# Pooled softmax in three exponentials, a normalisation in four pieces that sorts the heads, and a newly written order

## The chip, the cores and the metric

One Trainium2 chip, one core of it. The metric is the device time of one execution in microseconds (us), the median of several runs. Engines are named as the profile names them: PE is TensorE (matmuls), PEld its weight loads, DVE is VectorE, ACT is ScalarE, POOL is GpSimd, SP is SyncE, which here only issues DMAs.

## The reference

Eight heads of attention over 576 positions, for 8 batches, in two branches that are added; the sum goes through a gated feed-forward layer.

```python
# attention, head_dim 64, factor 4
q_d = q.reshape(B, H, Sd, 4, D).mean(axis=3)      # k_d, v_d likewise: 144 pooled rows
out_d = softmax(q_d @ k_d.T / 8) @ v_d            # pooled branch
out_up = np.repeat(out_d, 4, axis=2)
mask = np.abs(pos[:, None] - pos[None, :]) < 4    # local branch: a band of 7
out_local = softmax(where(mask, q @ k.T / 8, -1e9)) @ v
x = (out_up + out_local)                          # 8 x 576 x 512
# feed-forward with token shift
x_prev = shift of x by one position
xk = mu_k * x + (1 - mu_k) * x_prev;  xr = mu_r * x + (1 - mu_r) * x_prev
v = np.maximum(xk @ w_k, 0) ** 2 @ w_v            # w_k 512 x 1024, w_v 1024 x 512
out = sigmoid(xr @ w_r) * v                       # w_r 512 x 512
```

The weights and mu come as 64-bit floats and are turned into 32-bit floats on the chip, each as a high part and a low part (`weight_scale`, `weight_shift`, `weight_tail`, `weight_sign`, `weight_high`, then `weight_diff` and `weight_left`, or `weight_low` on GpSimd).

## The kernel before

Attention goes by **tiles**: tile n is a pair of heads of one batch, 32 tiles in all, four to a batch. A tile's q and k are loaded (`load_raw`), brought into the layout with head_dim on the partitions (tiles 0 to 4 by `flip` on PE, with copies out by `turn_part` on ACT and DVE; later ones by DVE), pooled on GpSimd (`pool_q`, `pool_k`) and multiplied: `score_both` for tiles 0 to 4, `run_pe` from tile 5 on, which also does the value products of the tile before. The pooled scores and the local scores of a tile share one PSUM tile of two banks, the board `ps_a`, of which there is one: the next tile's scores can start only when all readers of the last one are through (`score_top`, `down_top` on DVE, `down_exp` on ACT).

The **pooled probabilities** of a tile are 2 heads x 144 queries x 144 keys. Queries 0 to 127 of the two heads and the last 16 of each are spread over three column blocks of the board; the two halves of its first and third block belong to different heads. `down_exp` (line 744) takes five exponentials, four over 64 partitions, so that in `ad` each block of columns holds one head; each also sums its rows. `down_sum` forms reciprocals on DVE, `down_norm` (line 755) multiplies on GpSimd in place. Then `ad` is transposed into `adT`: for tiles 0 to 7 by PE (`down_turn`, lines 763 to 767, one PSUM bank) with one copy out on ACT (`down_copy`, line 792); from tile 8 on by DVE in 32 x 32 blocks (`down_blocks`, line 773) and by DMA through DRAM (`down_out`, `down_in`). `av_pe` (or `run_pe`) multiplies `adT` with the pooled v.

The **feed-forward layer** goes by 18 chunks of 256 rows: `k_pe` (x w_k), `r_pe` (x w_r) and `v_pe` (the squares x w_v) are the large matmuls on PE; between `k_pe` and `v_pe` stand `k_part`, `k_sum`, `k_relu`, `k_high`, `k_low` on ACT, DVE and GpSimd. Chunk 0 needs all four tiles of batch 0, whose mix with the row before is done by `mix_pe`, `mix_split`, `mix_rest`. So the program has a **first stretch**, up to the first `k_pe` (line 974), in which tiles 0 to 3 and the weights are prepared, and a long rest in which chunks and tiles are woven together.

The **order** of all 2,417 steps is written out in a string, `ORDER`: each engine gets its steps in just that order, SP's DMA issues among them. `Plan.arrange` reads the string, and with durations given in the `add(...)` calls works out which PSUM bank each step uses, where matmuls without use (`keep_warm`, line 483) are put into PE's gaps, and for which earlier transfer an early DMA issue has to wait (`landed_before`, with `QUEUE`). These durations set no time on the chip, but by way of banks, filling and waits they shape the program.

Of the kernel before, what the change touches and what calls it, by code (L numbers as in the profile page):

```python
# [52 lines left out]
494A1k3c1s3d1$0$3=3e3s1l1t3f1%1&3u3>404B4C1a413#4D1(1b3v1c4s4E4t4F4u1)1m1*3$1,1v4G4I4M4Q4J3%3w4K4H1-1w1x1y5l4N
1d5n4L3t3x1.1/3y5i5,3j5k5-5.3&5m4O4P4R4S3(4T1e4v5o5p3)4w5u4x4Y4g4U4V4k4c4W1z1!4X4l3z4m4Z3*3!1:1;4y4d4z6I5j6J5r
5$5w5s4a5%4b4e4f4n4*5t5v5:6M5<4!4#5x4h4+4$5y5;5z5q4%5&5(5)4o554p5!565*5>1f5=4i4j4,5#5+61574&4-6B6j4q4.4r4<6O6C
6N656D4(6E4)4/62666P4:51585T6359676m6k606Q68694=4>6A6K6#6n6l6F6G6H6$5/5A644;52505S5U536o6q6p6S6y6L6z956c6W6&54
6R6d6!5C5D5G5K5V6X6(6Y6Z6e6r5H5E6T6a5W6f6s6g6*6%6h6)6U6V5F6t6b6i6u6v5X5I5L5M6w5J5N6+6,6-6.785Y5Z5O969293949X9V
9Y6x6/7198797A7B7C7D5P7G5Q7E5R977F725a5b5c7H7I737J6:746;7K6<7N7T7O7U7V7P5d7x7Z7l7L5B9y9U5e5g9v99759E9A767Q7R7S
7M6=777W7a867X9B7b7c879H7Y6>7f7d9C9D7g9F7h9N7e7-9W9z5f709G9Z88898A7i7j7m7n8D9I9O7k7o9P9Q7/7p7q9J8E7,7.9a9b7:9R
9S9K9c7r7;7%7s8B9T8F7t7y7u7<9d7z8C7v7w8G9L7&7!7(9o7)7#7*8H9!7$9i8J8P7=8K9e9f8L7+9g8b7>8V80A4A7A89M9p9$9w9hCS9q  # L60
9r9s9#8Q8M9j9k9t9%8N8R8O9u9&8I9l9x8S8T8W8U9m8X9<8c9(8Y8Z818d839=9)8a8h8e8f8i8j8+8k8lAA8n9,828gA6A59n9+AC8o9>8p
A08mA9A19-9.A2AB8,8z8-8t9*A39/AD9:AOAP8u8q8rAEAF8v8wAG8sAV8xAWAQ8!AXAYAZAdCU8#Ae8$Af8yARAaAIAb8.8/8)8:8(8;Ag8%
# [1349 lines left out]
```

## Time and profile before

| | us |
|---|---|
| median of 3 runs (681.16 to 681.96) | 681.39 |
| the profiled execution | 680.52 |
| its span, first to last instruction | 678.7 |
| PE busy in the span | 648.4 |
| first `k_pe` starts at | 81.52 |

The span lacks 1.82 us of the profiled execution's time, which lie around it; the median is 0.87 us above that execution. A PE record of this kernel is one pass of a matmul: a 32-bit product shows as two records (x2 in the count), a product of rounded operands (fp32r) as one. [...]

### The profile page before, as it was taken

The numbers are of one execution on the slowest core, as the hardware profiler recorded it, in microseconds if no ns is written. First come the engines' busy times: TensorE is split into PE (matmuls) and PEld (weight loads), VectorE is DVE, ScalarE is ACT, GpSimd is POOL, SyncE is SP. The second block draws the span as 40 slices with busy tenths as digits, with TensorE's granted clock in tenths as the row PEclk, the third lists the DMA queues.
The fourth block names the chain that finished last, engine by engine and source line by source line (L and its number), as shares of the span: only waits on it lengthen the run. The fifth ranks groups of instructions, "written<-read, shape, count | busy, mean of one in ns | idle before, by whom it ended". The sixth has DMA issues, their size and how long they took to land.

```text
span 678.7 us, 19065 instructions
## 1 busy us (share of the span) xinstructions
PE 648.4 (96%) x7292; PEld 539.6 (79%) x7292; DVE 514.7 (76%) x1044; ACT 488.9 (72%) x1275; POOL 284.2 (42%) x375
## 2 busy tenths in 40 slices
PE   5886999999999999989999999999998999999997
PEld 5565898987888888868788888888887888888885
DVE  3888765679997998898978878789799876664312
ACT  3887697678886887958686777688777686765543
POOL 5435587664354456452444444544445242000000
PEclk9897999999999999999999999999999999999999
DMA  8999434646554457645245444664564133000101
GB/s 290 242 297 201 79 72 72 147 91 137 105 98 82 87 138 149 145 82 125 56 95 121 96 89 100 140 132 101 108 137 96 34 88 80 1 17 1 46 1 62
DMA packets 251580, 71.97 MB, mean 106 GB/s; under 512 B 224346, under 2 KB 243170, under 8 KB 251490
## 3 DMA queue, kind: packets, MB, share of 16 engines
q1 hardware_dynamic: 251490, 70.76, 46.3%
q8 instruction: 57, 0.93, 0.6%
q14 instruction: 33, 0.27, 0.2%
HBM read 56.85 MB, written 13.86 MB: 104 GB/s over the span
## 4 chain that ended last, share of the span: by engine, by line
PE 72%; DVE 12%; ACT 7%; SPq 2%; issue 2%; DMA 2%; POOL 1%; DVEq 0%; POOLq 0%; ACTq 0%
PE acc L1040 23%; PE ps_g L978 14%; PE ps_r L1024 13%; PE ps_g L980 7%; PE ps_v L802 5%; PE ps_a L654 2%; ACT ad L744 2%; PE ps_g L974 2%; PE ps_a L723 1%; DVE kk L991 1%; PE ps_a L659 1%; DVE kl L1013 1%; DVE xk L957 1%; DVE dx L957 1%; PE ps_w L476 1%
## 5 line engine op out<-in xcount | busy, mean ns | idle before, releaser
L1040 PE MATMUL acc<-wv,kh 128*128 128x512 f32 x578 | 182.8, 397 | 0.4 <-DVE sig L1050 0.2
L978 PE MATMUL ps_g<-xk,wk 128*128 128x512 f32 x512 | 140.7, 396 | 3.8 <-DVE xk L966 3.2
L1040 PEld LDWEIGHTS acc<-wv,kh 128*128 128x128 f32 x578 | 101.0, 189 | 17.9 <-DVE sig L1050 0.7
L978 PEld LDWEIGHTS ps_g<-xk,wk 128*128 128x128 f32 x512 | 92.8, 188 | 26.4 <-issue 4.5
L1040 PE MATMUL acc<-wv,kl 128*128 128x512 f32 x289 | 113.3, 392 | 0.0
L1024 PE MATMUL ps_r<-wr,xr 128*128 128x512 f32 x432 | 105.8, 394 | 2.9 <-DVE kk L991 2.9
L1024 PEld LDWEIGHTS ps_r<-wr,xr 128*128 128x128 f32 x432 | 79.9, 188 | 21.2 <-DVE kk L991 1.9
L1013 DVE TENSOR_TENSOR kl<-kk,kh 128x256 fp32r<-128x256 f32 x119 | 61.7, 521 | 33.6 <-ACT kh L1006 33.5
L980 PEld LDWEIGHTS ps_g<-xk,wk 128*128 128x128 f32 x512 | 78.1, 188 | 11.0
L991 DVE TENSOR_TENSOR kk<-ps_g,kk 128x256 f32<-128x256 f32 x128 | 52.5, 413 | 44.0 <-ACT kk L986 43.7
L986 ACT ACTIVATE kk<-ps_g 128x256 f32<-128x256 f32 x128 | 47.6, 377 | 51.5 <-PE ps_g L980 30.3
L980 PE MATMUL ps_g<-xk,wk 128*128 128x256 f32 x512 | 81.1, 281 | 0.0
L1000 ACT ACTIVATE kk<-kk 128x256 f32<-128x256 f32 x128 | 52.3, 412 | 37.7 <-DVE kk L991 37.1
L744 ACT ACTIVATE ad<-ps_a,mxd 64x144 f32<-64x144 f32 (+1 forms) x160 | 60.2, 376 | 11.1 <-DVE mxd L736 6.5
L682 POOL TENSOR_TENSOR sm<-sm,mx 128x384 f32<-128x384 f32 x28 | 25.7, 917 | 99.4 <-DVE mx L677 91.0
L1006 ACT ACTIVATE kh<-kk 128x256 fp32r<-128x256 f32 x144 | 60.2, 418 | 7.2 <-PE acc L1040 2.7
L1040 PEld LDWEIGHTS acc<-wv,kl 128*128 128x128 f32 x289 | 54.2, 188 | 13.1 <-DVE kl L1013 0.5
L1013 POOL TENSOR_TENSOR kl<-kk,kh 128x256 fp32r<-128x256 f32 x25 | 18.8, 754 | 108.1 <-ACT kh L1006 107.9
L1005 ACT ACTIVATE kk<-kk 128x256 f32<-128x256 f32 x144 | 59.3, 412 | 2.1
L618 POOL TENSOR_TENSOR tk<-kz 64x288 f32<-64x288 f32 (+1 forms) x56 | 43.3, 773 | 28.8 <-DVE kz L562 9.3
L697 POOL TENSOR_TENSOR sm<-sm,ssum 128x384 f32<-128x384 f32 x32 | 29.2, 911 | 54.5 <-DVE ssum L693 50.3
L802 PE MATMUL ps_v<-bd,vw 64*64 64x48 f32 x1536 | 51.7, 219 | 0.0
(134 smaller groups left out, 1273.7 us busy)
## 6 DMA issues: line engine op xcount, KB each, us to landing
vw<-in_v_dram SPq DMA_DIRECT2D x126, 96.0 KB, 2.7
out_dram<-sig SPq DMA_DIRECT2D x35, 256.0 KB, 2.2
v<-in_v_dram SPq DMA_DIRECT2D x32, 256.0 KB, 3.0
qraw<-in_q_dram SPq DMA_DIRECT2D x108, 72.0 KB, 2.5
kraw<-in_k_dram SPq DMA_DIRECT2D x108, 72.0 KB, 2.4
wk<-in_moe_w_k_dram SPq DMA_DIRECT2D x8, 512.0 KB, 4.8
wv<-in_moe_w_v_dram SPq DMA_DIRECT2D x8, 512.0 KB, 5.3
keys<-blocks SPq DMA_DIRECT2D x96, 40.0 KB, 1.9
```

The source lines that it names most:

```text
L744: nc.scalar.activation(ad[h, x, 0:144], ps[h, t, :], AF.Exp, scale=1.0 / 128, bias=mx[h, t:t + 1], accum_out=sd[h, x:x + 1])
L802: nc.tensor.matmul(pv[r][64 * e:64 * e + 64, cols], lhs, rhs, start=(i == 1), stop=(i == NG + 1 + (r != e)))
L978: nc.tensor.matmul(ps, w_k_part(p, f, 0), x[:, :, p, :], start=(p == 0), stop=False)
L980: nc.tensor.matmul(ps[:, 0], w_k_part(p, f, 1), x[:, 0, p, :], start=False, stop=(p == NP - 1))
L986: nc.scalar.activation(kk, ps[:, 1], AF.Copy)
L991: nc.vector.tensor_tensor(out=kk, in0=ps[:, 0], in1=kk, op=ALU.add)
L1000: nc.scalar.activation(kq[c, f], kq[c, f], AF.Relu)
L1005: nc.scalar.activation(kk, kk, AF.Square)
L1006: nc.scalar.activation(kh, kk, AF.Copy)
L1013: eng.tensor_tensor(out=kl, in0=kk, in1=kh.bitcast(F32), op=ALU.subtract)
L1024: nc.tensor.matmul(ps, x[:, y, p, P * t:P * t + P], ws[f"r{p}"][:, w, :], start=(m == 0), stop=(m == len(mm) - 1))
L1040: nc.tensor.matmul(accs[c][t][:, h], x[:, P * t:P * t + P], ws[f"v{f}"][:, w, h], start=(f == 0 and m == 0), stop=(f == NF - 1 and m == 2) ...
```

## The change

1. `down_exp` takes three exponentials, each over all 128 partitions, with the heads left as they stand in the board.
2. `down_norm` takes four multiplications on GpSimd in place of one, and writes to another tile, `an`, where they put the heads in order (64 partitions x 2 x 144, twice 64 x 144, 128 x 144). `clear` zeroes `an` in place of `ad`.
3. `down_turn` (tiles 0 to 7) uses full 128-column turns and two PSUM banks: 4 transposes of 128 x 128 and 3 small matmuls, where 8 matmuls were, 4 of them on 64 columns. `down_copy` takes three activations in place of one.
4. Durations of the plan are changed, and `ORDER` is another.
5. A wait of `store_mul` on the gate is spelled out for the last chunk's halves.

```diff
-        for t, x, h in ((0, 0, slice(0, 64)), (0, 1, slice(64, P)), (2, 1, slice(0, 64)), (2, 0, slice(64, P)), (1, 2, slice(0, P))):
-            nc.scalar.activation(ad[h, x, 0:144], ps[h, t, :], AF.Exp, scale=1.0 / 128,
-                                 bias=mx[h, t:t + 1], accum_out=sd[h, x:x + 1])
+        for t, x in enumerate((0, 2, 1)):
+            nc.scalar.activation(ad[:, x, :], ps[:, t, :], AF.Exp, scale=1.0 / 128,
+                                 bias=mx[:, t:t + 1], accum_out=sd[:, x:x + 1])
...
-        sd, x = st[n]["sd"], ad[:, :, 0:144]
-        nc.gpsimd.tensor_tensor(out=x, in0=x, in1=sd[:, :, None].broadcast_to([P, 3, 144]), op=ALU.mult)
+        sd = st[n]["sd"]
+        lo, hi = slice(0, 64), slice(64, P)
+        for h, to, of in ((lo, slice(0, 2), slice(0, 2)), (hi, 0, 1), (hi, 1, 0), (slice(0, P), 2, 2)):
+            x, y, z = an[h, to, 0:144], ad[h, of, :], sd[h, of] if of != 2 and h is lo else sd[h, of:of + 1]
+            z = z[:, :, None].broadcast_to([64, 2, 144]) if h is lo else z.broadcast_to([x.shape[0], 144])
+            nc.gpsimd.tensor_tensor(out=x, in0=y, in1=z, op=ALU.mult)
...
-        for e in range(2):
-            nc.tensor.matmul(ps[:, e, 0:128], ad[:, e, 0:128], idn, start=True, stop=True)
-            nc.tensor.matmul(ps[:, e, 128:144], ad[:, 2, 0:128], lasts[e], start=True, stop=True)
-        for e in range(2):
-            nc.tensor.matmul(ps[64 - 64 * e:128 - 64 * e, 2, 0:128], ad[:, e, 80:144], idn, start=True, stop=True)
-            nc.tensor.matmul(ps[64 - 64 * e:128 - 64 * e, 2, 128:144], ad[:, 2, 80:144], lasts[e], start=True, stop=True)
+        for x, ps in enumerate(d["ps_t"]):
+            o = [(16, 80), (0, 0)][x == 0]
+            for e in range(2):
+                nc.tensor.transpose(ps[:, e, 0:128], flat[:, DP * e + o[e]:DP * e + o[e] + 128], idn)
+            if x == 0:
+                nc.tensor.matmul(ps[:, :, 128:144], flat[:, 2 * DP:2 * DP + 128], lasts, start=True, stop=True)
+            else:
+                for e in range(2):
+                    nc.tensor.matmul(ps[:, e, 128:144], flat[:, 2 * DP + o[e]:2 * DP + o[e] + 128], lasts[:, e], start=True, stop=True)
...
-        nc.scalar.activation(adT, st[n]["ps_t"], AF.Copy)
+        for x, ps in enumerate(st[n]["ps_t"]):
+            for e in range(x + 1):
+                h = slice(0, P) if x == 0 else slice(64 - 64 * e, P - 64 * e)
+                nc.scalar.activation(adT[h, 0:2] if x == 0 else adT[h, 2], ps[h] if x == 0 else ps[h, e], AF.Copy)
...
-011<0X001=242625290f2T2U212X02092y0H2V1S0P0.1>201L2W2z1E173B0Y0Z2207230g0h272R2Z282a0i0a0j0b2Y2d082b0A2B2I2c2C
+001<2101221=0X2T2U0f0224092X2y2z0H1>1L0.1E0P202V3B230Y250827282a2Z0g260Z0a2Y0b030h2c0i0j292B2$2d2R070c2b2f040A
```

Where the new order moves things, by the built programs:

PE up to and at tile 2's scores. `kraw` and `qraw` with `ps_f` are the flips of k and q; `ps_a<-kd,qd_71` opens the scores of an even tile, `qd_72` of an odd one; `ps_w` are weights. Before, at tile 2 (the row ahead is the end of tile 1's value products):

```order
L802 MATMUL ps_v<-bd,vw 64x48 x9
L553 MATMUL ps_f<-idn,kraw 64x64 x18
L935 MATMUL ps_m<-xt,diag 128x256 x4
L553 MATMUL ps_f<-idn,qraw 64x64 x18
L717 MATMUL ps_a<-kd,qd_71 128x144
L649 MATMUL ps_a<-mask_77,idn 128x192 x2
```

Now, from the end of tile 0's scores to the opening of tile 1's:

```order
L724 MATMUL ps_a<-kd,qd_71 64x144 x4
L554 MATMUL ps_f<-idn,qraw 64x64 x18
L554 MATMUL ps_f<-idn,kraw 64x64 x18
L477 MATMUL ps_w<-w_244,idn 128x512
L478 MATMUL ps_w<-wk_339,nidn 128x512
L477 MATMUL ps_w<-w_251,idn 128x512
L478 MATMUL ps_w<-wv_365,nidn 128x512
L718 MATMUL ps_a<-kd,qd_72 128x144
```

Tile 2's k was flipped behind the value products of tile 1; now it is flipped ahead of the scores of tile 1, and tile 2's scores stand directly behind the value products of tile 0. All of PE's steps ahead of the first `k_pe` are the same ones as before, without the 9 filling matmuls, which the new program doesn't have.

SP at the program's start. `wk` and `wv` are weights of 512 KB, `qraw` and `kraw` 288 KB each (tiles 0, 1, 2 in turn), `idn` and `mask_77` constants of 64 and 96 KB. Before:

```order
L502 DMA qraw<-in_q_dram 128x576
L447 DMA wk_100<-in_moe_w_k_dram 128x1024
L390 DMA mask_77<-in_band_dram 128x6x32
L391 DMA idn<-in_ident_dram 128x128
L502 DMA kraw<-in_k_dram 128x576
L447 DMA wv_132<-in_moe_w_v_dram 128x1024
L502 DMA qraw<-in_q_dram 128x576
L502 DMA kraw<-in_k_dram 128x576
L395 DMA bd<-in_moe_mu_k_dram 4x128
L396 DMA bd<-in_moe_mu_r_dram 4x128
L447 DMA wk_180<-in_moe_w_k_dram 128x1024
L502 DMA qraw<-in_q_dram 128x576
```

Now:

```order
L392 DMA idn<-in_ident_dram 128x128
L503 DMA qraw<-in_q_dram 128x576
L503 DMA kraw<-in_k_dram 128x576
L448 DMA wk_126<-in_moe_w_k_dram 128x1024
L503 DMA qraw<-in_q_dram 128x576
L503 DMA kraw<-in_k_dram 128x576
L448 DMA wv_132<-in_moe_w_v_dram 128x1024
L396 DMA bd<-in_moe_mu_k_dram 4x128
L397 DMA bd<-in_moe_mu_r_dram 4x128
L448 DMA wk_156<-in_moe_w_k_dram 128x1024
L503 DMA qraw<-in_q_dram 128x576
L503 DMA kraw<-in_k_dram 128x576
```

The constants (the mask is one row above) go first, no weight stands ahead of tile 0's q and k, and tile 2's k follows its q at once; before it came 14 rows later.

GpSimd at tile 0's normalisation; `sm` is the local branch, `tk`, `kd` the pooling of k, `v` and `vd` that of v. Before:

```order
L697 TENSOR_TENSOR sm<-sm,ssum 128x384
L618 TENSOR_TENSOR tk<-kz_76 128x288
L619 TENSOR_TENSOR kd<-tk 128x144
L755 TENSOR_TENSOR ad<-ad,sd 128x3x144
L627 TENSOR_TENSOR v_82<-v_82 128x3x128
```

Now:

```order
L698 TENSOR_TENSOR sm<-sm,ssum 128x384
L761 TENSOR_TENSOR an<-ad,sd 64x2x144
L761 TENSOR_TENSOR an<-ad,sd 64x144 x2
L761 TENSOR_TENSOR an<-ad,sd 128x144
L619 TENSOR_TENSOR tk<-kz_75 128x288
```

One multiplication became four, and tile 2's pooling of k (`kz_75`) stands right behind them.

## Rows read from the trace of the kernel before

**Rows 1.** The page: span, PE's busy time, DMA throughput in 40 slices of 17 us.

```profile
span 678.7 us, 19065 instructions
...
PE 648.4 (96%) x7292; PEld 539.6 (79%) x7292; DVE 514.7 (76%) x1044; ACT 488.9 (72%) x1275; POOL 284.2 (42%) x375
...
GB/s 290 242 297 201 79 72 72 147 91 137 105 98 82 87 138 149 145 82 125 56 95 121 96 89 100 140 132 101 108 137 96 34 88 80 1 17 1 46 1 62
```

**Rows 2.** Waits of PE: line, what it waited for, us, times, longest.

```profile
PE ps_f L553 <- DMA kraw<-in_k_dram: 7.3, 1, 7.3
PE ps_a L717 <- POOL kd L619: 3.6, 1, 3.6
PE ps_g L978 <- DVE xk L966: 3.2, 4, 1.4
...
PE ps_r L1024 <- DVE kk L991: 2.9, 2, 1.5
```

**Rows 3.** Busy time by stretch: length, engines, granted clock, DMA share, GB/s; sum to 82.

```profile
54.00:58.00 4.00, 2.08 (x10) 1.64 (x10) 3.90 (x11) 3.92 (x13) 1.93 (x3) 0.50 0.96 296
...
sum 82.00, PE 63.84 PEld 49.66 DVE 59.04 ACT 56.90 POOL 40.45; mean PE 2.78 PEld 2.16 DVE 2.57 ACT 2.47 POOL 1.76
```

**Rows 4.** The same view, one stretch in the long rest.

```profile
280.00:320.00 40.00, 37.58 (x310) 30.73 (x303) 37.25 (x66) 29.87 (x73) 14.29 (x17) 1.00 0.55 112
```

**Rows 5.** Timeline of PE: start, us, line, operation, records, idle before in brackets.

```profile
14.61 0.48 PE L717 MATMUL ps_a<-kd,qd 128*128 128x144 f32 x2 [0.33 <-ACT qd L610]
...
24.98 0.68 PE L717 MATMUL ps_a<-kd,qd 128*128 128x144 f32 x2
...
28.14 0.49 PE L763 MATMUL ps_t<-idn,ad 128*128 128x128 f32 x2
...
29.59 1.20 PE L483 MATMUL ps_x<-nidn 128*128 128x512 f32 x4
...
42.05 1.11 PE L553 MATMUL ps_f<-idn,kraw 64*64 64x64 f32 x32
...
46.51 0.51 PE L717 MATMUL ps_a<-kd,qd 128*128 128x144 f32 x2
...
55.92 0.84 PE L717 MATMUL ps_a<-kd,qd 128*128 128x144 f32 x2 [3.57 <-POOL kd L619]
...
81.52 10.28 PE L974 MATMUL ps_g<-xk,wk 128*128 128x256 f32 x84
```

**Rows 6.** Timeline of ACT: two exponentials of tile 0 and its one copy out.

```profile
19.65 0.38 ACT L744 ACTIVATE ad<-ps_a,mxd 64x144 f32<-64x144 f32 x1 [0.48 <-DVE mxd L736]
...
20.13 0.38 ACT L744 ACTIVATE ad<-ps_a,mxd 64x144 f32<-64x144 f32 x1
...
29.71 0.53 ACT L792 ACTIVATE adT<-ps_t 128x432 f32<-128x432 f32 x1 [2.00 <-PE ps_t L767]
```

**Rows 7.** Timeline of GpSimd: tile 1's pooled k, tile 0's normalisation.

```profile
22.16 0.43 POOL L619 TENSOR_TENSOR kd<-tk 128x144 f32<-128x144 f32 x1
22.59 0.91 POOL L755 TENSOR_TENSOR ad<-ad,sd 128x432 f32<-128x432 f32 x1
```

**Rows 8.** Groups by form: line, engine, shapes, count, busy us, mean ns, idle before.

```profile
L1013 DVE TENSOR_TENSOR kl<-kk,kh 128x256 fp32r<-128x256 f32 x119 | 61.7, 521 | 33.6 <-ACT kh L1006 33.5
...
L618 POOL TENSOR_TENSOR tk<-kz 64x288 f32<-64x288 f32 x48 | 36.0, 750 | 14.2 <-DVE kz L591 6.3 <-DMA keys<-blocks 4.0 <-DVE mxd L736 1.7
```

**Rows 9.** Line 1013 alone: duration min/median/max in ns, first and last start.

```profile
L1013 DVE TENSOR_TENSOR kl<-kk,kh x119: 361/426/1123, 112.1 to 670.9; 128x256 fp32r<-128x256 f32 x119
```

**Rows 10.** SP's issues: start, us; k of tiles 2 and 3.

```profile
25.00 0.40 SPq L502 DMA_DIRECT2D kraw<-in_k_dram  x1
...
33.72 0.33 SPq L502 DMA_DIRECT2D kraw<-in_k_dram  x1
```

**Rows 11.** Tile ad between 388 and 425 us: normalisations, and the transposes that read them.

```profile
L755 POOL TENSOR_TENSOR ad<-ad,sd x2: 910/952/995, 394.2 to 413.6; 128x432 f32<-128x432 f32 x2
L773 DVE STREAM_TRANSPOSE blocks<-ad x2: 662/670/678, 403.3 to 422.3; 128x480 f32<-128x480 f32 x2
```

More of the change, by code (lines that the diff above doesn't have):

```diff
@@ L53 @@
[L53 to L62, printed above, removed]
@@ L114 @@
     TAIL = dict(PE=0.16, DVE=0.08, ACT=0.095, POOL=0.04, SP=0.0)
-    WAIT = dict(PE=0.055, DVE=0.035, ACT=0.035, POOL=0.1, SP=0.1)
+    WAIT = dict(PE=0.16, DVE=0.035, ACT=0.035, POOL=0.1, SP=0.1)
     SAME = 0.033
@@ L118 @@
     TABLES = dict(down_exp=1, score_exp=1, gate=2)
-    ISSUE, LAND = 0.6, 1.1
-    GROW = dict(DVE=1.03, ACT=1.02, POOL=1.06, SP=1.1)
-    QUEUE = 6.0
+    ISSUE, LAND = 0.6, 2.2
+    GROW = dict(DVE=1.02, ACT=1.02, POOL=1.04, SP=1.08)
+    QUEUE = 4.5
     SLACK = 1.0
@@ L421, in clear @@
     def clear():
-        for x in (*kzs, *qTs, *qds, *v4s, side, ad):
+        for x in (*kzs, *qTs, *qds, *v4s, side, an):
             nc.gpsimd.memset(x, 0.0)
@@ L1094, in prepare @@
             for nm in "qk":
-                add("PE", 1.1, R - 9.5, flip, n, nm, r=[f"{nm}raw{n}", "idn"], new=[(f"{nm}flip{n}{x}", "bank") for x in range(2)])
+                add("PE", 1.35, R - 9.5, flip, n, nm, r=[f"{nm}raw{n}", "idn"], new=[(f"{nm}flip{n}{x}", "bank") for x in range(2)])
                 for x in range(2):
-                    add(*(("ACT", 0.45) if (nm, x) in FLIPACT else ("DVE", 0.45)), R - 9, turn_part, n, nm, x,
+                    add(*(("ACT", 0.68) if (nm, x) in FLIPACT else ("DVE", 0.68)), R - 9, turn_part, n, nm, x,
                         r=[f"{nm}flip{n}{x}"], w=[(f"{nm}T{i}", x)])
@@ L1115, in down_steps @@
         add("DVE", 0.8, R1 - 14, down_top, n, r=[ps], w=[f"mxd{n}"], lock=ps)
-        add("ACT", 2.0, R1 - 13, down_exp, n, r=[ps, f"mxd{n}"], w=["ad"], lock=ps)
+        add("ACT", 1.2, R1 - 13, down_exp, n, r=[ps, f"mxd{n}"], w=["ad"], lock=ps)
         add("DVE", 0.36, R1 - 10, down_sum, n, r=["ad"], w=[f"sd{n}"])
-        add("POOL", 0.91, R1 - 9, down_norm, n, r=[f"sd{n}"], w=["ad"])
+        add("POOL", 1.75, R1 - 9, down_norm, n, r=[f"sd{n}", "ad"], w=["an"])
         if n < EARLY:
-            add("PE", 1.0, R1 - 7, down_turn, n, r=["ad"], new=[(f"pst{n}", "bank")])
-            add("ACT", 0.5, R1 - 6, down_copy, n, r=[f"pst{n}"], w=["adT"])
-        else:
-            add("DVE", 0.62, R1 - 7, down_blocks, n, r=["ad"], new=[(f"blk{n}", "dtmp")])
-            add("SP", 3.0, R1 - 6.5, down_out, n, r=[f"blk{n}"], w=[f"keys{n % 2}"], dma=1.9)
+            add("PE", 0.95, R1 - 7, down_turn, n, r=["an"], new=[(f"pst{n}{x}", "bank") for x in range(2)])
+            add("ACT", 0.9, R1 - 6, down_copy, n, r=[f"pst{n}0", f"pst{n}1"], w=["adT"])
+        else:
+            add("DVE", 0.67, R1 - 7, down_blocks, n, r=["an"], new=[(f"blk{n}", "dtmp")])
+            add("SP", 3.0, R1 - 6.5, down_out, n, r=[f"blk{n}"], w=[f"keys{n % 2}"], dma=1.5)
     def score_steps(n):
@@ L1253, in s_part @@
                 for i in range(n):
-                    add("DVE", 0.67 / n, where["v7"] - 6, store_mul, c, t, i, r=[f"acc{c}.{t}"],
+                    add("DVE", 0.67 / n, where["v7"] - 6, store_mul, c, t, i, r=[f"acc{c}.{t}"] + ([f"sig{c}.{t}"] if n > 1 else []),
                         w=[f"sig{c}.{t}"] if n == 1 else [(f"sig{c}.{t}", i)])
@@ L1293, in attention_moe @@
         score_steps(n)
-        add("PE", 1.35, after(n), av_pe, n, **av_of(n))
+        add("PE", 1.5, after(n), av_pe, n, **av_of(n))
         value_steps(n)
@@ L1326, in attention_moe @@
                     prepare(EARLY)
-                    add("PE", 0.9, at_run[n] + 1, down_alone, EARLY, **join(down_of(EARLY), dict(new=[("psx", "att")])))
+                    add("PE", 1.4, at_run[n] + 1, down_alone, EARLY, **join(down_of(EARLY), dict(new=[("psx", "att")])))
                     down_steps(EARLY, "psx")
```

106 lines of the change are left out of this document (59 added, 47 removed).

## The prediction

> **What bounds the kernel now.** First the page: PE is busy 648.4 of 678.7 us [rows 1]. A quicker ACT or a slower GpSimd counts only where PE waits, and all waits together are 30 us. So the next view is PE's list of waits [rows 2], and then PE's timeline, to see where they lie [rows 5]. There are three places. (a) The start: 7.3 us until the first q and k have landed. (b) The first stretch, up to the first `k_pe` at 81.52. By the sum of its stretches PE is busy 63.84 us of the first 82 [rows 3], so some 18 us are idle, 7.3 of them the start and about 10.7 inside; the longest gap inside is 3.57 us ahead of tile 3's scores at 55.92 [rows 5], where PE waits for GpSimd's pooled k. [...] (c) The rest, 81.52 to 678.7: 597.2 us with only some 7 us of waits (3.2 on `xk`, 2.9 on `kk` and smaller ones [rows 2]) and the last store's way out. The rest is bound by PE's work, which the change leaves nearly as it is. The first stretch is a chain of dependent steps, and it is there that an order can gain much.
>
> In PE's timeline the scores of tiles 0 to 3 open at 14.61, 24.98, 46.51 and 55.92, and the first `k_pe` stands at 81.52 [rows 5]: spacings of 10.4, 21.5, 9.4 and 25.6 us. The odd one is the second. Tile 2's k was issued at 25.00 [rows 10] and flipped at 42.05 [rows 5], behind the value products of tile 1, because SP's and PE's rows stand so.
>
> **Part 1, the new order, first stretch.** I follow the five pieces of that sum through the new queues with durations of this trace.
>
> - *Start.* Ahead of tile 0's k there were 1,248 KB (q, a weight, two constants, k), now 736. At 290 GB/s in the first slice [rows 1] the 512 KB less are 1.8 us, so PE starts at about 5.5 in place of 7.3. Score 0 opens as much earlier, and by another 1.5 us at most, since `turn_sign` and a weight have moved behind tile 0 on ACT: 11.3 (bounds 10.8 and 13).
> - *Score 0 to 1.* Tile 1 waits for the board, and its last reader is `down_exp`, 0.48 us from one exponential to the next [rows 6]. Two fewer save 0.96 us. The weight steps around it are much the same: 10.4 becomes 9.4. Opens at 20.7.
> - *Score 1 to 2.* Tile 2's q and k are flipped before score 1 now, so only the board holds score 2 back, as it did score 1: about 9.4 us for 21.5. Opens at 30. Its loads come in time: up to tile 2's k 3.4 MB are asked for, and the first slice alone moves 290 GB/s x 17 us = 4.9 MB [rows 1].
> - *Score 2 to 3.* Here part of that comes back. ACT and DVE must still do the weights and diagonals that filled the gap. On ACT, 19 steps stand between tile 1's and tile 2's exponentials, which I put at 13 us, and tile 3's q is copied out behind them and pooled (0.67 + 0.43 us) after that: about 17 us, against 9.4. Opens at 47. Tile 3's k (issued at 33.72 before [rows 10]) has 8.0 MB up to it now; two slices move 290 and 242 GB/s [rows 1], so 8.0 MB are there by about 30.
> - *Score 3 to the first `k_pe`.* Readers of the board on DVE, exponentials, reciprocals, four multiplications, turn, copies, value products, scores of tile 4, the last mix: the steps are those of before, with 0.96 us less on ACT, 1.1 more on GpSimd (part 2) and two more small copies. Before, PE held tile 3's turn back behind value products and a weight that came late; these stand clear now. I take 20.5 us for 25.6.
>
> Sum: 11.3 + 9.4 + 9.4 + 17 + 20.5 = 67.6. [...] A walk like this leaves out small waits, so I add 2.5 and take **70.0** (bounds 65 and 80) for 81.52: **-11.5 us**.
>
> **Part 2, the pieces.** ACT: two exponentials fewer, 0.48 us each [rows 6], in 32 tiles: 31 us of its 489 [rows 1]; worth nothing by itself where PE doesn't wait. GpSimd: one multiplication of 0.91 us [rows 7] becomes one like the 64 x 288 of line 618, 0.75 [rows 8], and three like the pooled k's last step, 0.43 [rows 7]: 2.04 us, so +1.1 us in each tile, 36 us in all. Bounds: +0.9 if neighbours overlap, +1.5 if they are slowed. In the first stretch this cancels ACT's gain; later it is hidden by slack. In the late trace the normalisation starts at 394.2 and its reader, the transpose, at 403.3 [rows 11]: 8.1 us between end and use; the next pair is alike (413.6, 422.3). Copies out of early turns: one of 0.53 [rows 6] becomes three; about +0.6 in 8 tiles, in ACT's time freed. The turn on PE took 29.59 - 28.14 = 1.45 us [rows 5]; the new one has 4 transposes, which no row shows, and 3 small products: between 1.0 and 1.9, and I take no change. Banks: a turn asks for two of six, for 2 to 3 us, at nothing.
>
> GpSimd's added time has one more way to cost. Line 1013's subtraction on DVE takes 426 ns in the median, 521 in the mean and up to 1,123 [rows 8, 9], and GpSimd works beside it: 0.095 x 119 = 11 us lost there. If twice that is lost over all such lines with 284 us of GpSimd [rows 1], 36 us more cost some 3 us of DVE, and PE sees a part. [...]
>
> **Part 3, the rest.** PE's work after the first `k_pe` is the same, and so is the tail. Of the 7 us of waits there I expect new ones in place of old: DVE is at 37.25 of 40 us in 280 to 320, where PE loses 2.4 [rows 4]. The new order asks for `r_pe` of chunk 0 about 4 us earlier than before while GpSimd has two weights more to do than at that point before, of 1.3 us each. I take **+1 us** (bounds -4 and +6).
>
> **Sum.** 680.52 - 11.5 + 1 = 670.0 for a profiled execution; the median before is 0.87 above it: **671.0**.
>
> **The rivals.**
> 1. *The first stretch shrinks, and half is lost again in chunks 0 and 1*, because weights and loads that the gap gave time for are late: PE then waits on GpSimd's `weight_low` or on k's low parts. For it: GpSimd gets fuller. Against: 40.45 of 82 us are its load now [rows 3]. 677, range 674 to 680.
> 2. *Nothing is gained, since loads bound the first stretch.* For it: 290, 242, 297 and 201 GB/s in the first four slices [rows 1], then 79: all of the weights come in that time, and tiles asked for earlier push weights back. Against: the bytes up to tiles 2 and 3, above. 681, same.
> 3. *Slower: the four multiplications come onto each tile's path.* If the new order puts the transpose or the turn right behind the normalisation, 1.1 us reach PE in 27 tiles (5 to 31): +30 us, or 701 with the gain of the start; it decides from where the 8.1 us of slack [rows 11] is used up, and it makes the kernel slower from 11 of these tiles on. [...]
> 4. *Better:* the first `k_pe` stands near 65, with PE at its full clock throughout: 665.
>
> **How the numbers follow.** Forecast (666 to 675) 0.60; rival 1 0.17; rival 2 0.07; rival 3 0.10; rival 4 0.06. The range 664 to 680 holds the forecast and rivals 1 and 4. Within 0.2% (680.0 to 682.8) is about what a measurement can't tell from no change. Faster: 0.60 + 0.06 + 0.16 = 0.82; same: 0.07 + 0.01 = 0.08; slower 0.10.
>
> **What would show it.** Right: the first `k_pe` (now line 987) at 66 to 74; scores of tiles 2 and 3 near 30 and 47; three exponentials of 0.48 us spacing; normalisation of about 2 us; PE idle in the rest under 12 us. Wrong: tile 2's scores at 35 or later (the step on the board or on loads fails); PE's waits on line 761 or on `adT` summing to more than 3 us (rival 3); waits on GpSimd's weights after the first `k_pe` (rival 1); the granted clock at 0.50 for longer than before.

## The result, and the profile after

The changed kernel takes **673.21 us** (median of 4 runs, 672.02 to 676.97), the kernel before in the same comparison 681.56 (681.16 to 681.96): a ratio of 0.9887, 95% interval 0.9847 to 0.9927. The prediction was 671.0, range 664 to 680. The profiled execution took 672.69.

The page of the changed kernel, beside [rows 1]: ACT is 33.3 us less busy, GpSimd 37.2 more, DVE the same to 1.2 us.

```profile
span 670.6 us, 18917 instructions
...
PE 641.2 (96%) x7235; PEld 537.6 (80%) x7235; DVE 515.9 (77%) x1044; ACT 455.6 (68%) x1161; POOL 321.4 (48%) x471
...
GB/s 280 248 273 157 194 84 70 136 73 126 76 93 145 148 108 122 122 107 96 105 143 42 159 41 106 128 141 135 57 72 123 100 64 86 1 33 0 32 13 51
```

Busy time by stretch, up to the first `k_pe` and from there on (columns as in [rows 3]; the granted clock is a share of PE's full speed); first the kernel before, then the changed one.

```profile
0.00:81.50 81.50, 63.37 (x1277) 49.18 (x1277) 58.57 (x121) 56.40 (x149) 39.95 (x64) 0.92 0.85 231
81.50:678.70 597.20, 584.99 (x6015) 490.38 (x6015) 456.09 (x924) 432.46 (x1127) 244.29 (x312) 1.00 0.42 89
```

```profile
0.00:72.70 72.70, 58.49 (x1244) 46.70 (x1245) 54.09 (x114) 51.18 (x137) 42.73 (x77) 0.93 0.91 240
72.70:670.60 597.90, 582.66 (x5993) 490.90 (x5991) 461.79 (x930) 404.37 (x1026) 278.72 (x395) 1.00 0.44 91
```

The whole gain is in the first stretch, 8.8 us; the rest is 0.7 us longer. PE's timeline of the changed kernel, beside [rows 5] (line 718 opens a tile's pooled scores, 987 is the first `k_pe`):

```profile
5.50 2.19 PE L554 MATMUL ps_f<-idn,qraw 64*64 64x64 f32 x36 [5.50 <-DMA qraw<-in_q_dram]
...
12.86 0.51 PE L718 MATMUL ps_a<-kd,qd 128*128 128x144 f32 x2
...
21.97 0.41 PE L718 MATMUL ps_a<-kd,qd 128*128 128x144 f32 x2
...
30.70 0.48 PE L718 MATMUL ps_a<-kd,qd 128*128 128x144 f32 x2 [0.47 <-issue]
31.02 0.81 PE L650 MATMUL ps_a<-mask,idn 128*128 128x192 f32 x4
31.77 0.84 PE L660 MATMUL ps_a<-kz,qT 64*32 64x32 f32 x75
35.96 0.43 PE L660 MATMUL ps_a<-kz,qT 64*32 64x32 f32 x21 [3.35 <-issue]
...
52.43 0.48 PE L718 MATMUL ps_a<-kd,qd 128*128 128x144 f32 x2 [0.22 <-ACT qd L611]
...
72.72 0.47 PE L987 MATMUL ps_g<-xk,wk 128*128 128x256 f32 x1
```

The spacings are 9.1, 8.7, 21.7 and 20.3 us. In the middle of tile 2's local scores, between the 75th and the 76th of 96 equal records of matmuls that wait for nothing, PE stands still for 3.35 us, and "issue" means that the profile shows no reason. PE's list of waits has such stops as its largest entry:

```profile
PE ps_a L660 <- issue: 6.3, 4, 3.4
PE ps_f L554 <- DMA qraw<-in_q_dram: 5.5, 1, 5.5
PE ps_g L991 <- DVE xk L979: 3.6, 4, 1.3
PE ps_a L724 <- issue: 1.4, 1, 1.4
```

The kernel before has 0.4 us of them. The busy time by stretch of the changed kernel shows what follows the stop: the granted clock is at 0.50 from 36 to 44; DVE does nothing from 36 to 38, GpSimd nothing from 36 to 42.

```profile
34.00:36.00 2.00, 0.04 (x6) 0.04 (x9) 1.09 (x2) 2.00 (x8) 1.27 (x2) 0.83 1.17 269
36.00:38.00 2.00, 2.00 (x51) 1.94 (x53) 0.00 (x0) 1.28 (x3) 0.00 (x0) 0.50 1.29 139
38.00:40.00 2.00, 2.00 (x26) 1.88 (x23) 0.97 (x2) 0.08 (x1) 0.00 (x0) 0.50 0.81 141
40.00:42.00 2.00, 2.00 (x9) 1.48 (x7) 1.97 (x5) 1.23 (x4) 0.00 (x0) 0.50 0.86 281
42.00:44.00 2.00, 2.00 (x21) 0.92 (x23) 1.75 (x4) 0.89 (x3) 1.54 (x3) 0.50 0.97 278
44.00:46.00 2.00, 2.00 (x51) 1.92 (x46) 0.70 (x1) 1.28 (x4) 1.92 (x3) 0.61 0.95 293
```

So there are two questions: is the gain the order's alone, as the prediction has it, and what are the stops?

### The profile page after: what moved, and what is told of

Read it like the earlier page. It is cut to its first block, busy times and chain, and to the rows that moved or that the text cites. A ratio compares the mean times of both kernels' runs of the same rounds, so it can differ in the third digit from the quotient of the medians.

```text
span 670.6 us, 18917 instructions
## 1 busy us (share of the span) xinstructions
PE 641.2 (96%) x7235; PEld 537.6 (80%) x7235; DVE 515.9 (77%) x1044; ACT 455.6 (68%) x1161; POOL 321.4 (48%) x471
## 4 chain that ended last, share of the span: by engine, by line
PE 47%; DVE 29%; ACT 7%; issue 5%; POOL 4%; DMA 4%; SPq 3%; DVEq 0%; POOLq 0%; ACTq 0%
PE acc L1053 16%; PE ps_g L991 9%; PE ps_r L1037 8%; PE ps_g L993 5%; PE ps_v L815 3%; DVE kl L1026 3%; DVE kz L592 3%; DVE kk L1004 2%; POOL an L761 2%; DVE dx L923 2%; PE ps_g L987 2%; SPq L509 1%; DVE xt L902 1%; DMA qraw<-in_q_dram 1%; DVE qT L578 1%
## 5 line engine op out<-in xcount | busy, mean ns | idle before, releaser
L1037 PE MATMUL ps_r<-wr,xr 128*128 128x512 f32 x432 | 104.2, 391 | 0.1
L1026 DVE TENSOR_TENSOR kl<-kk,kh 128x256 fp32r<-128x256 f32 x119 | 59.5, 503 | 30.6 <-ACT kh L1019 30.5
L761 POOL TENSOR_TENSOR an<-ad,sd 64x144 f32<-64x144 f32 (+2 forms) x128 | 68.2, 543 | 28.9 <-DVE sd L752 24.4
L683 POOL TENSOR_TENSOR sm<-sm,mx 128x384 f32<-128x384 f32 x28 | 27.9, 998 | 71.4 <-DVE mx L678 69.6
L698 POOL TENSOR_TENSOR sm<-sm,ssum 128x384 f32<-128x384 f32 x32 | 28.1, 877 | 45.5 <-DVE ssum L694 22.2
```

The lines of the kernel that those rows point to most:

```text
L761: nc.gpsimd.tensor_tensor(out=x, in0=y, in1=z, op=ALU.mult)
L1026: eng.tensor_tensor(out=kl, in0=kk, in1=kh.bitcast(F32), op=ALU.subtract)
L1037: nc.tensor.matmul(ps, x[:, y, p, P * t:P * t + P], ws[f"r{p}"][:, w, :], start=(m == 0), stop=(m == len(mm) - 1))
```

## Experiments on the order and the pieces

**The pieces alone.** The old order with the three exponentials, four multiplications and the new turn. The durations of the plan stay the changed kernel's, so the string is another one than in the kernel before, though each engine gets its steps in that kernel's order; only the fillings differ (13 records, 9 before).

```diff
-ORDER = """ 001<2101221=... (of the changed kernel)
+ORDER = """ 011<0X001=0f2T... (each engine's steps as in the kernel before)
```

> Three exponentials, four multiplications and the new turns and copies, each engine in the order of before. My theory: the pieces alone are worth nothing, since ACT gets 1 us shorter per tile and GpSimd 1 us longer: 679 to 684, first k_pe at 80 to 83. Rival (31 us less on ACT are what gives the gain): 672 to 676.

Measured: 687.38 us, ratio 1.0093 (1.0078 to 1.0108). A miss: the pieces aren't worth nothing in the old order, they cost 6 us. The first `k_pe` stands at 81.88, so the loss lies behind it: 603.7 us for 597.2. DVE's waits show where, in the kernel before, with the pieces alone, and in the changed kernel:

```profile
DVE blocks L773 <- POOL ad L755: 4.7, 4, 1.8
```

```profile
DVE blocks L783 <- POOL an L761: 12.7, 8, 3.0
```

```profile
DVE blocks L783 <- POOL an L761: 1.5, 3, 0.8
```

The DVE transposes of tiles 8 to 31 wait 8.0 us more for the longer normalisation. In the new order they hardly wait. What PE sees of it is the busy time behind the first `k_pe`, to be held against the row of the kernel before above:

```profile
81.90:685.60 603.70, 588.46 (x5995) 491.31 (x5995) 458.15 (x924) 404.56 (x1023) 275.14 (x396) 0.99 0.42 88
```

Half of the 6.5 us are waits of PE there (10.4 us for 7.1), the other half is busy time (588.5 for 584.9): the granted clock, which doesn't fall there in the kernel before, is at 0.50 from 146.0 to 149.4 and from 528.3 to 531.7, soon after waits of PE of 1.8 us (on `xt`) and 2.7 us (on `xk`). Stops are not the reason; counted as in the next section they sum to 0.5 us there. Worked out from the trace, tile by tile, the time from the normalisation's end to its transpose is under 1 us in 7 of 24 tiles before (median 2.4), in 12 with the pieces alone (0.8), in 8 in the changed kernel (2.3). With the new order and the short normalisation, the next run, it is 1 tile, and the median 4.6: the new order leaves the normalisation more room.

**The order alone.** The new order with five exponentials, one multiplication, old turn, one copy.

```diff
-        for t, x in enumerate((0, 2, 1)):
+        for t, x, h in ((0, 0, slice(0, 64)), (0, 1, slice(64, P)), ...):
...
-        for h, to, of in ((lo, slice(0, 2), slice(0, 2)), (hi, 0, 1), (hi, 1, 0), (slice(0, P), 2, 2)):
+        nc.gpsimd.tensor_tensor(out=an[:, 0:3, 0:144], in0=ad, in1=sd[:, :, None].broadcast_to([P, 3, 144]), op=ALU.mult)
```

> The new order with five exponentials that sort the heads, one multiplication, and the turns and the copy of before. My theory: the gain is the order's, 671 to 677, first k_pe at 71 to 76, tile 2's scores at 30 to 33. Rival (the pieces give the gain, or the order gains only with them): 679 to 684.

Measured: 679.29 us (10 runs, 675.39 to 683.91), ratio 0.9977 (0.9951 to 1.0004). A miss again: alone the order gains 2 us at most. Its DVE waits:

```profile
DVE sd L751 <- ACT ad L745: 10.1, 9, 2.6
DVE ssum L692 <- ACT sm L687: 8.8, 9, 1.9
```

In the changed kernel the first of these is 1.7 us. So DVE waits for ACT, which has two exponentials more to do in each tile. The profiled execution took 683.50, 4 us over the median. Tile 2's scores open at 34.41 there and the first `k_pe` stands at 79.93, both later than expected; its stops before that (6.6 us) are no more than half a microsecond over those of the changed kernel (6.1), so they are not what separates the two.

So the two parts don't add up. Order alone -2, pieces alone +6, both -8: some 12 us lie between the sum and the whole. The waits above make it plausible that the order fits the pieces' durations.

**New up to tile 5's scores, old from there.**

```diff
-ORDER = """ (new)
+ORDER = """ (new up to run_pe of tile 5, then the remaining steps in the old order)
```

> The pieces of the changed kernel; its order up to tile 5's scores, the old order from there on. Theory (first stretch and rest add up, and the rest of the old order does not suit the longer normalisation): first k_pe at 72 to 74, the rest 602 to 605 as with the pieces alone in the old order (603.7): 676 to 680 us. Rival (what the pieces lost in the old order was lost between the first k_pe and chunk 1 only, because of how the first stretch ended): rest 597 to 599, 671 to 674.

Measured: 684.67 us (679.94 to 688.15), ratio 1.0041 (1.0016 to 1.0066). The rival falls: the rest takes 607.3 us, and DVE's wait for the normalisation is 13.2 us, as with the pieces alone. The theory's numbers are too low all the same. The first `k_pe` stands at 75.2, not at 72 to 74, and the rest is 3.6 us longer than with the pieces alone: 1.8 in waits of PE (12.2 for 10.4), 1.7 in its busy time (590.1 for 588.5). Why isn't explained.

**The old turn and copy** in the changed kernel.

```diff
-            for e in range(2):
-                nc.tensor.transpose(ps[:, e, 0:128], flat[:, DP * e + o[e]:DP * e + o[e] + 128], idn)
...
+            nc.tensor.matmul(ps[:, e, 0:128], an[:, e, 0:128], idn, start=True, stop=True)
...
+        nc.scalar.activation(adT, st[n]["ps_t"], AF.Copy)
```

> The changed kernel, new order, three exponentials and four multiplications, but the old turn of tiles 0 to 7 in one bank (8 matmuls) with one copy out. Theory (turn and copies are worth nothing; the new order needs the shorter exponentials): 672 to 675 us, first k_pe at 72 to 74. Rival (the new order alone lost because of the old turn, as tile 0's value products waited 2.0 us for adT there): 677 to 681, first k_pe at 76 or later.

Measured: 672.89 us, ratio 0.9886 (0.9859 to 0.9912), against 0.9887: turn and copies are worth nothing, as predicted. The first `k_pe` stands at 75.5, between the theory's 72 to 74 and the rival's 76, and the rest is 2.8 us shorter than in the changed kernel (595.1 for 597.9) and has no stop. So one profile's first `k_pe` doesn't tell the total. What the new order needs are the exponentials and the normalisation; the two were not taken apart.

**The normalisation twice**, in tiles 8 to 31.

```diff
             nc.gpsimd.tensor_tensor(out=x, in0=y, in1=z, op=ALU.mult)
+            if n >= EARLY:
+                nc.gpsimd.tensor_tensor(out=x, in0=y, in1=z, op=ALU.mult)
```

> The changed kernel, with GpSimd's four multiplications of the normalisation issued twice in tiles 8 to 31 (the second time the same values again); nothing is left out. In the changed kernel's trace the time from the normalisation's end to the DVE transpose that reads it is under 1 us in 8 of these 24 tiles and under 2.1 us in 10. Theory (no slack in a third of the tiles): 2.1 us more in each tile puts about 17 us of new waits on DVE; with the pieces alone in the old order 8.0 us of such waits went with 6 us of time, so +13 us: 686 us, range 682 to 690, DVE's waits on line 761 above 14 us. Rival (slack of about 8 us, as the prediction read it from one pair of tiles): 673 to 675. Second rival (GpSimd stops DVE while it multiplies): DVE's busy time grows by 20 us or more, its waits do not.

Measured: 705.22 us (703.89 to 710.26), ratio 1.0367 (1.0325 to 1.0408). Slack of 8 us is out of the question. DVE's wait is what the theory said, the time is more than twice it:

```profile
DVE blocks L785 <- POOL an L763: 20.1, 11, 3.2
```

Other steps are late as well: DVE's waits in `up`, 6.1 us in the changed kernel, are 13.5 here. The rest, 625.7 us, is 27.8 longer, and PE's busy time there shows why the time grows by more than the waits:

```profile
82.60:708.20 625.60, 592.49 (x5993) 495.73 (x5991) 460.76 (x929) 403.50 (x1024) 330.09 (x491) 0.99 0.41 86
```

PE waits for 28.1 us in place of 10.0, and is busy for 592.5 in place of 582.7, with the granted clock at 0.50 in five stretches there, in the changed kernel in one. The profiled execution took 710.26, 5 us over the median; its first `k_pe`, by the same instructions, stands at 82.5, with stops of 9.7 us before it (6.1 in the changed kernel), so part of its length is chance. The second rival falls for the total: DVE is busy for 515.6 us with GpSimd at 373.4, and for 514.7 with GpSimd at 284.2 in the kernel before.

**One multiplication on ACT**, with the 24 matmuls of the next section.

```diff
+            if of == 2:
+                nc.scalar.activation(x, y, AF.Copy, scale=sd[:, 2:3])
+            else:
-            nc.gpsimd.tensor_tensor(out=x, in0=y, in1=z, op=ALU.mult)
+                nc.gpsimd.tensor_tensor(out=x, in0=y, in1=z, op=ALU.mult)
```

> The same, and the last of the four multiplications of the normalisation (128 x 144) on ACT, scaled by the reciprocal sums, in place of GpSimd. It makes GpSimd's part some 0.45 us shorter in 32 tiles and ACT's 0.4 longer. Theory (the normalisation's end is what DVE's transpose waits for in a third of the tiles): 8 tiles gain up to 0.45 us: 664 to 668. Rival (ACT's queue: the activation waits for the reciprocals and everything behind it on ACT with it): 670 to 676, ACT's waits for sd above 5 us.

Measured: 668.94 us (667.87 to 672.76), no better than the 668.02 without it and between the ranges of theory and rival; ACT's waits for `sd` are 4.7 us. In the profiled execution (672.76) the rest takes 594.0 us against 597.4, but with the old turn it took 595.1 without any change to the normalisation, so a gain isn't shown. In the first stretch PE's turns wait for ACT, and there are stops of 5.9 us against 0.4:

```profile
PE ps_t L777 <- ACT an L762: 3.2, 3, 2.0
```

ACT for tiles 8 to 31 alone wasn't tried.

## Experiments on PE's stops

The page has a DMA queue by the name of instruction. The changed kernel's rows (packets, MB, share):

```profile
q1 hardware_dynamic: 251490, 70.76, 48.1%
q8 instruction: 57, 0.93, 0.6%
```

57 packets of 16 KB, and PE with its weight loads and semaphore waits has 14,627 records: 0.93 MB over these come to 64 bytes for a record, so 256 records for a packet. Counted so, all the larger stops of the changed kernel (0.86, 3.55, 1.73, 0.88 and 1.75 us between two records, at records 449, 1217, 2497, 3521 and 4033) have a record number that leaves 193 when divided by 256, and PE resumes 1.3 to 1.5 us after a packet's end. The view of the queues between 32.9 and 34.5, within the stop of 3.35 us, has the packet, among loads that keep the engines at 94.5%:

```profile
q1 hardware_dynamic: 216, 0.57, 94.5%
q8 instruction: 1, 0.02, 5.7%
```

From the record times (us; a stop here is the distance between two records' starts):

```
kernel, record      block before entered   packet            last record   next record
before, 1217        34.05                  36.80 to 37.73    42.47         42.47
changed, 1217       29.09                  32.96 to 34.42    32.41         35.96
changed, 2497       66.71                  67.36 to 69.36    68.96         70.68
changed, 4033       123.22                 123.87 to 125.34  125.02        126.77
```

In the first 60 us of the changed kernel a packet starts 1.4 to 3.9 us after PE enters the block before, as if it were asked for then; later in the run, by the same count, between 1.6 us after that and 4.1 ahead of it. Scores and value products are small matmuls: ahead of these five stops 256 records last 1.8 to 4.1 us, and PE resumes 2.9 to 6.9 us after it entered the block before, the longest of these beside the loads of the first 60 us. At the changed kernel's other borders, where 256 records last 3.3 us and more, two records are at most 0.23 us apart. Sums of these stops over 0.3 us before 140 us, where PE waits for nothing else: 0.6 us in the kernel before, 8.8 in the changed one. The theory is then that the place of the block borders in the program counts, and that matmuls without use ahead of PE's first step, in the time in which it waits for q and k anyway, move them (four records each).

```diff
+    def code_ahead():
+        z = cp.tile([P, 32], F32, name="z")
+        nc.vector.memset(z, 0.0)
+        ps = pp.tile([P, 512], F32, tag="b0", name="ps_z", bufs=1)
+        for _ in range(24):
+            nc.tensor.matmul(ps[0:32, 0:32], z[0:32, :], z[0:32, :], start=True, stop=True)
+
+    in_order(code_ahead)
     for t in emitted:
```

**24 of them (96 records), in the changed kernel:**

> The changed kernel with 24 small matmuls on zeros put ahead of PE's first step, where PE waits 5.5 us for data anyway: 96 more records (24 products, two passes, each a weight load and a matmul). Nothing else changes. My theory, formed from the trace of after: the gaps inside tile 2's scores (3.35 us), tile 0's (0.67), tile 4's (1.44) and two of 0.7 and 1.55 later, all of which the view puts down to issue, are PE waiting for its own instructions: each stands where the count of PE's records is 193 over a multiple of 256, and a 16 KB packet of the instruction queue comes in just before PE goes on. With 96 records more the multiple falls elsewhere, at moments at least 4 us apart: those gaps go (under 1 us in all inside scores), tile 3's scores open at 49 or earlier in place of 52.4, the first k_pe at 67 to 70 in place of 72.7, total 667 to 670. Rival (the gaps are waits for data or for the board): they stay at tile 2's scores, total 673 as after.

Measured: 668.99 us (667.85 to 669.30), ratio 0.982 (0.9806 to 0.9835). The total is in the range; how it came about is taken up behind the control. **64 of them (256 records, one whole block)**, as a control:

> The control of the run before: 64 small matmuls, 256 records, so the count modulo 256 is as in the changed kernel. My theory: the gap in tile 2's scores is back at the same place (2.5 to 4.5 us), total 672 to 675. If the small matmuls helped in another way (a warmer PE at the start, a shifted start), this run gains as much as the one with 24, 667 to 670.

Measured: 675.97 us, ratio 0.9927 (0.991 to 0.9943). The stops are back at the same matmuls, in tile 2's scores with 21 records left:

```profile
35.96 0.32 PE L660 MATMUL ps_a<-kz,qT 64*32 64x32 f32 x21 [1.07 <-issue]
```

But this one is smaller than the 2.5 to 4.5 us expected, and the total is above the range. The 64 matmuls last until 7.98 us, so the first flip and the first `k_pe` (76.69) are late: as a control of the total it isn't clean. With 24 the stop is still at record 1217, now 48 matmuls earlier in the same scores, which is the 96 records:

```profile
36.68 0.80 PE L660 MATMUL ps_a<-kz,qT 64*32 64x32 f32 x69 [3.65 <-issue]
```

(x69 are left here, 48 more than the 21.) That it would go was a miss: its packet began 8.8 us after PE entered the block before. Tile 3's scores (51.34) and the first `k_pe` (70.66) are later than expected too; that the total fits is in part luck. What has gone are the changed kernel's three later stops (1.73, 0.88 and 1.75 us, 4.4 together), and 4.2 us of the median. Of the profiled executions' difference, 3.4 us, 2.1 lie before the first `k_pe` and 1.3 behind it, and the mean granted clock of the first stretch is 0.98 in place of 0.93; so the time can't be put down to the three stops one by one.

**24 again**, later, in 4 runs; on record it is the same chip as the first time, so it tests the repetition and not another chip:

> The changed kernel with 24 matmuls without use ahead, as before: 667 to 671 us on this chip too, with runs closer together than those of the changed kernel. If the 668.99 was the first chip's alone: 672 to 674.

Measured: 668.02 us (667.29 to 669.19), ratio 0.9806 (0.9783 to 0.983). It is the fastest version here, and its runs lie within 2 us where those of the changed kernel lie within 5. In its profile the packet for record 1217 landed in time, the stops sum to 0.4 us, and the clock stayed up where the changed kernel's fell:

```profile
34.00:36.00 2.00, 1.50 (x44) 1.40 (x38) 2.00 (x5) 2.00 (x7) 1.92 (x4) 1.00 1.15 222
36.00:38.00 2.00, 1.52 (x12) 1.16 (x10) 1.97 (x6) 2.00 (x6) 0.28 (x1) 1.00 1.19 180
```

Yet against the first set of runs, whose profile has 5.8 us of stops, that is only 1.0 us, and the first `k_pe` is 0.9 earlier. In the first stretch the stop was largely hidden: without it PE waits for ACT instead, 2.05 us ahead of tile 3's scores, and the clock falls there (0.50 from 52 to 56).

```profile
49.56 0.48 PE L718 MATMUL ps_a<-kd,qd 128*128 128x144 f32 x2 [2.05 <-ACT qd L611]
```

**Fewer loads under way**, in the changed kernel.

```diff
-    QUEUE = 4.5
+    QUEUE = 3.0
```

> The changed kernel with QUEUE 3.0 for 4.5: fewer early loads under way at a time. PE's instructions come in blocks of 256 records by the queue named instruction; in the first 60 us a block's packet starts 1.9 to 8.8 us after the previous block was entered, later 0.1 to 1.6, and PE resumes 1.3 to 1.6 us after the packet's end. Theory (the packet waits behind the loads): with fewer loads ahead it starts about 1 us earlier, the stop at record 1217 shrinks from 3.4 us to under 2.5, the first k_pe stands at 70 to 72: 669 to 672 us. Rival (the loads themselves are what counts): loads land later, PE waits for q and k or weights instead, 674 to 678.

Measured: 678.39 us (674.06 to 681.07), ratio 0.9954 (0.9932 to 0.9975). Both are seen: the stop at record 1217 is 0.23 us, since its packet began after 2.03 us in place of 3.87; and the loads come later, as the page's throughput shows beside that of the changed kernel:

```profile
GB/s 230 236 246 195 179 144 40 131 96 108 93 83 139 150 123 120 107 102 122 83 145 59 140 54 108 126 144 137 51 71 122 98 72 86 1 33 0 32 11 52
```

PE now waits for the copies and pooling behind those loads (`adT` 3.2 us, `qd` 2.9, `an` 1.7), and the first `k_pe` stands at 77.1. The rival holds for the time.

**16 and 32 matmuls ahead in the kernel before**, which has nearly no stops: the theory must make it slower too.

> The kernel before, with 16 matmuls without use (64 records of PE) ahead of its first step, in the time in which it waits for the first q and k. Theory (PE stops where 256 records are used up faster than the next block is fetched; blocks begin at records 193, 449, 705 and so on, whatever work falls there): worked out from the record times of the kernel before, with 6.0 us from entering a block to the next one being there before 60 us, 4.3 until 75 and 3.4 after, the stops sum to 3.2 us in the kernel before and to 0.6 with 64 records more ahead: 678 to 681 us. Rival (matmuls ahead help or harm by themselves): the same as the next kernel, which has 32 of them.

> The same with 32 matmuls (128 records), which still end before q and k land. Theory: by the same working the stops sum to 10.5 us in place of 3.2, 5.8 of them before 78 us; with the changed kernel 5.8 us of stops less went with 4.2 us of time, so about +5: 684 to 689 us, the stops at records that leave 193 when divided by 256. Rival: no different from the kernel with 16 by over 1 us.

Measured: 679.83 us (ratio 0.9978, 0.9961 to 0.9996) with 16, 683.45 (1.0033, 1.0016 to 1.005) with 32: 3.6 us apart, and by their intervals one is faster and one slower than without. With 16 there is no stop over 0.3 us before 140 us. With 32 there are four, at records 705, 3265, 3777 and 4289, all 193 by 256, in PE's timeline:

```profile
20.15 0.58 PE L553 MATMUL ps_f<-idn,qraw 64*64 64x64 f32 x5 [2.08 <-issue]
...
101.80 0.33 PE L659 MATMUL ps_a<-kz,qT 64*32 64x32 f32 x23 [0.74 <-issue]
...
118.77 0.26 PE L659 MATMUL ps_a<-kz,qT 64*32 64x32 f32 x5 [1.19 <-issue]
...
137.97 0.25 PE L659 MATMUL ps_a<-kz,qT 64*32 64x32 f32 x4 [1.93 <-issue]
```

The first one is hidden (the first `k_pe` is at 80.9, with 16 at 80.6), the other three, 4.4 us between records, are paid: behind the first `k_pe` the run with 32 takes 602.2 us, the one with 16 takes 598.0. The sign and the places were right; the time is just below the expected 684 to 689. The working put too much into the early stops: 3.2 us in the kernel before, which has 0.6, and 10.5 with 32, which has 6.7.

## Why the prediction was right, and where it was not

- *Start, 5.5:* 5.50. *Score 0, 11.3:* 12.86, at the edge of its bounds (10.8 to 13). Only the earlier loads counted; of the further gain of up to 1.5 us nothing came.
- *Scores 0 to 1 and 1 to 2, 9.4 each:* 9.1 and 8.7. Flipping tile 2's q and k ahead of tile 1's scores did what the walk said: 21.5 became 8.7.
- *Score 2 to 3, 17:* 21.7, the step that failed. The walk followed data and queues; it had no term for PE's own instructions. 3.35 us are the stop, and behind it PE works at a granted clock of 0.50 from 36 to 44. In the run without that stop the step takes 18.0 (31.58 to 49.56), by ACT's chain, as predicted.
- *Score 3 to the first `k_pe`, 20.5:* 20.3, of which 1.4 are another stop. *First `k_pe`, 70.0:* 72.72; with 24 matmuls ahead 69.7 and 70.7. The walk's sum (67.6) is 5.1 us short, 4.7 of it in the step from score 2 to 3; the 2.5 added for small waits covered half.
- *Rest, +1:* +0.7. PE's waits there sum to 10 us, 2.2 of them stops; by its busy time PE is idle for 15.2 us (12.2 before), over the bound of 12. That the term came out is luck: with the pieces alone the rest is 6.5 us longer, with the order alone 4.6 (in a profiled execution 4 us over its median), and the prediction saw neither.
- *ACT, -31 us, and about +0.6 for the copies in 8 tiles:* -33.3. *GpSimd, +36:* +37.2. An exponential follows the next by 0.36 us, not 0.48, and the four multiplications take 2.05:

```profile
19.73 0.38 ACT L745 ACTIVATE ad<-ps_a,mxd 128x144 f32<-128x144 f32 x1
20.00 0.21 ACT L745 ACTIVATION_READ_ACCUMULATOR ad<-ps_a,mxd 128x1 f32 x1
20.09 0.38 ACT L745 ACTIVATE ad<-ps_a,mxd 128x144 f32<-128x144 f32 x1
```

```profile
23.40 2.05 POOL L761 TENSOR_TENSOR an<-ad,sd 64x288 f32<-64x288 f32 x4
```

- *"Later it is hidden by slack", 8.1 us [rows 11]:* wrong as a reason. Those two tiles have the third and fourth largest slack of 24; the median is 2.4 us and 7 tiles have under 1. In the old order the pieces cost 6 us. Part 2's zero came out right because the new order leaves the normalisation more room, which the prediction didn't have.
- *Rival 3* is therefore no phantom: its mechanism is at work in the old order, and twice the multiplications make 705 us. The prediction's second cost, DVE slower beside GpSimd, is at work too, but doesn't grow with the change. Worked out from the trace of the changed kernel, instruction by instruction: line 1013's subtraction (line 1026 now) takes 415 ns in the mean with no GpSimd instruction beside it, 401 where one begins later, and 647, at most 1,065, where GpSimd is in the midst of one when it starts (46 of 119). In the kernel before these are 418, 380 and 701 (44 of 119). One of the longest, GpSimd's instruction first:

```profile
312.00 0.83 POOL L698 TENSOR_TENSOR sm<-sm,ssum 128x384 f32<-128x384 f32 x1 [2.59 <-DVE ssum L694]
```

```profile
312.05 1.06 DVE L1026 TENSOR_TENSOR kl<-kk,kh 128x256 fp32r<-128x256 f32 x1
```

What holds the subtraction up isn't shown. The line's mean is shorter by the same view as [rows 8], 503 ns for 521; by the same count over DVE's instructions of all lines, an estimate, the time lost so is some 34 us in the kernel before and 35 in the changed one, 3.5 and 2.7 of it beside the normalisation. DVE's busy time grew by 1.2 us, not by the prediction's some 3.

```profile
L1026 DVE TENSOR_TENSOR kl<-kk,kh 128x256 fp32r<-128x256 f32 x119 | 59.5, 503 | 30.6 <-ACT kh L1019 30.5
```

- *Rival 2, loads:* the first stretch now moves 240 GB/s with the DMA engines at 0.91, and asking for less at once costs 5 us. Whether more from the loads would gain anything there isn't shown.

So the forecast's total was right, and the gain lies where it was forecast, in the first stretch. But the prediction put it down to the order alone, and alone the order gives 2 us. Two terms were lacking: the stops, whose shifting is worth 4 to 5 us, and the fit of order to pieces, which it counted as free.

## To carry to other kernels

Here the order was worth 8 us only with the pieces that it came with: measure slack over all tiles and not in one pair, and don't add up gains of an order and of pieces that were measured apart. The "issue" gaps on PE in the midst of equal small matmuls stood here at borders of 256 records, in the changed kernel the five largest (0.67 to 3.35 us): where such gaps show, count records, and try to shift the border with a few useless matmuls in time that is lost anyway (here 4 to 5 us for 24 of them). Stops behind the first `k_pe`, 4.4 us with 32 matmuls ahead in the kernel before, were paid (602.2 us for 598.0); in the first stretch, where PE would have waited for ACT, they were largely hidden (with 24 matmuls ahead, 5.8 us of stops in one profile and 0.4 in the other, and the first `k_pe` 0.9 us earlier). And a wait of PE can cost more than its length: with the pieces alone 3.3 us more of waits came with 3.5 us more of busy time, with the granted clock at 0.50 in two stretches of 3.4 us.

## What the runs showed of the hardware

- PE's instructions came in packets of 16 KB by a queue of their own (57 in the changed kernel), 256 records to a packet by the count above, about one block ahead. In the first 60 us of the changed kernel, where loads kept the DMA engines at 0.91, a packet started 1.4 to 3.9 us after the block before was entered, with 24 matmuls ahead one of them 8.8; afterwards between 1.6 us after it and 4.1 ahead of it. PE resumed 1.3 to 1.5 us after the packet's end. Stops over 0.3 us before 140 us sum to 0.6 us in the kernel before and to 8.8 in the changed one.
- A stop of 3.35 us was followed by 8 us at a granted clock of 0.50; one of 3.65 with 24 matmuls ahead by slices of 2 us at 0.89, 0.50 and 0.75. What makes the difference stays open. In the long rest, with the pieces alone, the clock was at 0.50 soon after waits of PE of 1.8 us (from 146.0) and 2.7 us (from 528.3).
- Line 1026's subtraction on DVE, of two operands in SBUF, took 415 ns in the mean with no GpSimd instruction beside it; 647, and up to 1,065, where GpSimd was in the midst of an instruction at its start (46 of 119); and 401 where GpSimd began later.
- The first stretch varies from profile to profile: the same instructions up to the first `k_pe` gave 72.7 in the changed kernel and 82.5 with the normalisation twice in later tiles, with 3.5 us more of stops, a second wait for q of 1.9 and 2.8 more for tile 3's pooled q.
